# An attention, expert-attention and mixing kernel on one core: one 128-row piece of the theta weights is handed to a later stage of the order

## The chip, the cores and the metric

The program runs on one core of one Trainium2 chip. The metric is the device time of the execution in microseconds; the median of three runs is compared. The core has TensorE (PE, with its weight loads shown apart as PEld), VectorE (DVE), ScalarE (ACT), GpSimd (POOL) and SyncE (SP), whose queue issues most of the transfers. Each engine works through its own instructions in the order in which they stand in its queue.

## The reference

Three layers follow one another, for 4 batches of 576 tokens and 512 channels:

```
x  = local attention of 8 heads of 64, each query sees the last 64 keys
x  = for each of 4 experts: causal attention over x, times wo[e]; each token takes its best 2 experts
theta = x @ w_theta
y  = w_tok_r @ (x * cos(theta)) + w_tok_i @ (x * sin(theta))
u  = x + y
out = u + max(u @ w_ch, 0)
```

The weights of the last layer (w_theta, w_tok_r and w_tok_i, w_ch) come as 64-bit floats, since they are scaled in the host's double precision; the kernel receives their bits and turns them into a pair of 32-bit numbers, high and low, whose sum carries the value.

## The kernel before

Batches 0 to 3 go through local attention (`phase_a`), the projections to queries, keys, values and gates (`qk`, `vg_gates`), expert attention (`attn(b, ep)`, ep being the pair of experts 0, 1 or 2, 3) and, last, the mixing layer (`theta`, `mix` or `mix7`, `channel`). While one batch is in `attn`, `phase_a` and `qk` of the next ones run between its pieces. `merge` interleaves generators: each yields a cost, and the one that has the smallest share of its total done goes next. For each batch there are two such merges, the first half with `attn(b, 0)` and the second with `attn(b, 1)`. The build then schedules each engine's order from what `merge` emitted, so that a piece that is emitted elsewhere also moves its neighbours.

The table `THS` says in which half of which batch a 128-row piece c of the theta weights is handed to `load_theta` (lines 830 to 836): entry 2b is the first half of batch b, entry 2b + 1 the second. `load_theta` takes two 128-row buffers of the tag `zc` (the raw 64-bit piece `w64t` of 512 KB, and the scratch `wtut`), and calls `load64` (lines 107 to 148), which issues for each piece, in this order of dependence:

- SP, L115: one transfer of the raw piece, queued behind the last key tile `kt`
- POOL, L124: the high words scaled; ACT, L129: the low words scaled
- DVE, L130: a shift; DVE, L136: sign bit and shifted bits joined, with `w64t` and `wtut` as its two inputs
- POOL, L138: the sum of the two parts as integers
- ACT, L146: the high result `wth`; DVE, L147: the low result `wtl`, with `wtut` and `wth` as inputs

The results are read by the matmuls of `fuse`, at 277 us of the profiled execution. Nothing else reads them.

Other lines that the prediction speaks of: `pool_mul` (L87), the POOL copies of queries into `QD` and of keys into `KA`; L279, the score matmuls `as` of local attention; L284 the masked reduction of `as` on DVE; L299 the POOL multiplication that normalises `ams`; L452 the masked reduction of expert scores on DVE; L469 the scaling of `bms` and its diagonal part `bpd`, on POOL or DVE; L480 and L486 the transposes `bpt` and `bdt` of these on PE; L484, L482 and L490 their copies to `bpT`. Names carry the batch first: `as200` is batch 2, head pair 0, group 0; `bms011` is batch 0, expert pair 1, tile 1.

Of the kernel before, what the change touches and what calls it, by code (L numbers as in the profile page):

```python
# [28 lines left out]
CT = ("tb", "bs")  # L29
WARM = 2  # L30
TK0 = 1
THS = [[], [0], [], [1], [2], [3], [], []]
NB = S // 64
NC = DM // P
BIG = 1.0e30
# [22 lines left out]
def kernel(ctx, tc, qT, kT, vw, consts, w_in, w_o, w_th, w_tk, w_ch, outT):  # L58
# [143 lines left out]
    def load_w(src, n, dst_h, dst_l, tag):  # L202
        for c in range(n):
            h, l = dst_h(c), dst_l(c)
            pool, home = (cp, "zc") if tag == "zc" or tag == "both" and c >= 2 else (bp, "bms")
            st = pool.tile([P, h.shape[1]], F32, tag=home, bufs=2, name=f"wst{c}")
            with tc.issue_after(last_load[0].ins):
                nc.sync.dma_start(st, src[c * P : (c + 1) * P])
            w = h.shape[1]
            eh, el = KN["WE"][{"zc": 2}.get(tag, 0 if w == W0 else 1)]  # L210
            cut = w * eh // 4
            if eh < 4:
                nc.scalar.copy(out=h[:, cut:], in_=st[:, cut:])
            if eh > 0:
                nc.vector.tensor_copy(out=h[:, :cut], in_=st[:, :cut])
            cut = w * el // 4
            if el < 4:
                nc.gpsimd.tensor_sub(out=l[:, cut:], in0=st[:, cut:], in1=f32(h[:, cut:]))
            if el > 0:
                nc.vector.tensor_sub(out=l[:, :cut], in0=st[:, :cut], in1=f32(h[:, :cut]))  # L220
            yield 0.1
# [284 lines left out]
    def wo(b):  # L506
        for n0, n1 in ((0, 320), (320, 576)):
            for m in range(NC):
                g = bank([P, n1 - n0], ("gggg", ("as", "ta", "g", "g"), ("as", "g", "ta", "g"))[KN["WB"][b]][m], f"x2{b}{m}{n0}")
                for c in range(2):  # L510
                    oh, ol = O[b, c]
                    mm3(g, woh[c][:, m * P : (m + 1) * P], wol[c][:, m * P : (m + 1) * P],
                        oh[:, n0:n1], ol[:, n0:n1], c == 0, c == 1)
                nc.scalar.copy(out=x2T[b][:, m, n0:n1] if b < 2 else xs[b][m // 2][:, m % 2, n0:n1], in_=g)
                if b > 1 and n1 == S and m % 2:
                    nc.sync.dma_start(xd[b][:, m - 1 : m + 1], xs[b][m // 2])
                yield 0.75
# [312 lines left out]
    def load_theta(cs):  # L830
        for c in cs:
            st = cp.tile([P, DM], U64, tag="zc", bufs=2, name=f"w64t{c}")
            tu = cp.tile([P, 2, DM], U32, tag="zc", bufs=2, name=f"wtut{c}")
            load64(0, st, tu, wth[:, c], wtl[:, c], w_th[c * P : (c + 1) * P],
                   1.0 / TWO_PI)
            yield 1.0
# [48 lines left out]
    for b in range(B):  # L885
# [5 lines left out]
        if b > 0:  # L891
            todo.append((KN["WO"][b - 1], wo(b - 1)))
        if THS[2 * b]:
            todo.append((KN["TW"][0] * len(THS[2 * b]), load_theta(THS[2 * b])))
        if b == 3:
# [21 lines left out]
        if KN["WOI"] == 2 * b + 1:  # L917
            todo.append((KN["CW"][6], load_w(w_o, 2, lambda c: woh[c], lambda c: wol[c], "zc")))
        if THS[2 * b + 1]:
            todo.append((KN["TW"][1] * len(THS[2 * b + 1]), load_theta(THS[2 * b + 1])))  # L920
        if b == 2:
# [93 lines left out]
```

## Time and profile before

| | us |
|---|---|
| median of 3 runs | 509.3 (507.8 to 509.64) |
| the profiled execution's own time | 506.32 |
| its span | 504.5 |
| PE busy in the span | 480.7 (95%) |
| PEld, DVE, ACT, POOL busy | 446.4, 373.6, 346.4, 328.4 |
| granted TensorE clock | 0.999 of full speed |

The profiled execution took 3.0 us less than the median of the runs. Busy shares are averages over the whole span; the stretch from 60 to 110 us, in which the change moves work, is read by itself in the section on the rows. A matmul's record covers its passage through the array and overlaps the next one's, so PE can show as busy while its order holds back; PEld shows such stretches better.

### The profile page before, as it was taken

The page shows a single profiled execution, that of the slowest core. Times are in us where ns is not written, and L with a number is a line of the kernel's source. Part 1 is how long each engine was busy: PE and PEld are TensorE (multiplying, and loading weights), DVE is VectorE, ACT ScalarE, POOL GpSimd, SP SyncE. Part 2 cuts the span into 40 slices and gives each one's busy share as a digit, 9 for nine tenths or more (in the row PEclk, how much of TensorE's full clock was granted, in tenths as well). Part 3 has the DMA queues.
Part 4 walks back from the last instruction along what each step waited for, and adds up shares of the span by engine and source line. Part 5 has one row for each costly group of instructions (what it writes and reads, how often), then busy time and mean ns, then how long its engine had stood idle before and what let it go on. Part 6 is the DMA issues. An engine that isn't in the chain of part 4 may idle for free.

```text
span 504.5 us, 12104 instructions
## 1 busy us (share of the span) xinstructions
PE 480.7 (95%) x4128; PEld 446.4 (88%) x4128; DVE 373.6 (74%) x1274; ACT 346.4 (69%) x1072; POOL 328.4 (65%) x455
## 2 busy tenths in 40 slices
PE   7798999999999999999999989999999999999997
PEld 5688888889998999988878778899998999999997
DVE  5766887865977868845897778987769948894942
ACT  7948787866787868858696797886177727652620
POOL 6758899764685772335784367579658926891770
PEclk9999999999999999999999999999999999999999
DMA  7564233431335342111246953231272044202002
GB/s 256 189 212 155 83 123 114 130 114 64 122 88 177 124 141 78 34 47 49 52 146 208 318 166 142 55 93 43 76 196 64 23 142 131 64 23 95 1 0 95
DMA packets 45470, 55.92 MB, mean 111 GB/s; under 512 B 6497, under 2 KB 34145, under 8 KB 45409
## 3 DMA queue, kind: packets, MB, share of 16 engines
q1 hardware_dynamic: 44544, 52.46, 33.1%
q10 hardware_dynamic: 864, 2.69, 1.5%
q8 instruction: 33, 0.54, 0.4%
q14 instruction: 29, 0.23, 0.2%
HBM read 43.34 MB, written 11.80 MB: 109 GB/s over the span
## 4 chain that ended last, share of the span: by engine, by line
PE 51%; DVE 20%; ACT 11%; POOL 9%; issue 5%; DMA 4%; SPq 0%; POOLq 0%; DVEq 0%; ACTq 0%
PE as L279 4%; PE bpt L480 3%; PE qk L100 2%; PE c L100 2%; DMA w64k<-in_dram 2%; PE qk L101 2%; PE apt L304 2%; PE c L102 2%; PE qk L102 2%; PE c L101 2%; ACT ams L292 2%; PE ao L159 2%; DMA wst<-in_dram 2%; PE bs L448 2%; DVE ang L656 2%
## 5 line engine op out<-in xcount | busy, mean ns | idle before, releaser
L292 ACT ACTIVATE ams<-ams,anm 128x128 f32<-128x128 f32 x144 | 56.6, 396 | 6.1 <-DVE anm L284 4.8
L299 POOL TENSOR_TENSOR ams<-ams,arc 128x384 f32<-128x384 f32 x48 | 40.1, 836 | 24.9 <-DVE arc L298 15.5
L87 POOL TENSOR_SCALAR QD<-qt 64x192 f32<-64x192 f32 x72 | 40.1, 557 | 19.1 <-PE as L279 11.6
L457 ACT ACTIVATE bms<-bms,bnm 64x64 f32<-64x64 f32 (+4 forms) x80 | 44.8, 562 | 9.3 <-DVE bnm L452 8.8
L279 PE MATMUL as<-kt,QD 128*128 128x128 f32 x288 | 41.9, 282 | 3.9 <-DVE anm L284 1.5
L284 DVE CUSTOM_DVE_ANT_0 ams<-as,cst 128x128 f32<-128x128 f32 x144 | 35.0, 284 | 11.5 <-PE apt L304 7.8
L279 PEld LDWEIGHTS as<-kt,QD 128*128 128x128 f32 x288 | 36.6, 193 | 7.4 <-ACT x0h L94 1.5
L452 DVE CUSTOM_DVE_ANT_0 bms<-bs,mb 64x64 f32<-64x64 f32 (+4 forms) x80 | 32.6, 424 | 7.5 <-PE bs L450 4.7
L469 POOL TENSOR_SCALAR bpd<-bms,bsm,gw 128x64 f32<-128x64 f32 (+1 forms) x47 | 21.9, 467 | 23.1 <-DVE bsm L462 10.6
L97 POOL TENSOR_TENSOR cu<-x2T,cu 128x288 fp32r<-128x288 f32 x32 | 29.1, 923 | 7.3 <-ACT cu L94 7.3
L100 PE MATMUL y<-wkh,z 128*128 128x288 f32 x108 | 32.1, 302 | 0.2 <-DVE x2T L694 0.2
L448 PE MATMUL bs<-KA,QS 128*128 128x288 f32 (+4 forms) x96 | 31.8, 340 | 0.4 <-DVE bnm L452 0.2
L101 PE MATMUL y<-wkl,z 128*128 128x288 f32 x108 | 31.9, 297 | 0.0
L102 PE MATMUL y<-wkh,z 128*128 128x288 f32 x108 | 31.3, 297 | 0.0
L768 POOL TENSOR_TENSOR x2T<-x2T,u 128x288 f32<-128x288 f32 x20 | 16.6, 839 | 21.3 <-DVE u L779 11.1
L480 PE MATMUL bpt<-cst,bms 128*128 128x128 f32 x160 | 27.6, 278 | 2.9 <-POOL bms L469 1.8
L648 ACT ACTIVATE ang<-th,magic 128x256 f32<-128x256 f32 x36 | 16.7, 466 | 17.9 <-PE th L102 17.5
L656 DVE TENSOR_TENSOR ang<-xk,ang 128x512 f32<-128x512 f32 x32 | 21.7, 684 | 8.2 <-ACT ang L653 6.2
L450 PE MATMUL bs<-KL,QS 128*128 128x288 f32 (+4 forms) x96 | 27.6, 295 | 0.1
L292 ACT ACTIVATION_READ_ACCUMULATOR ams<-ams,anm 128x1 f32 x144 | 27.5, 191 | 0.0
L820 DVE SCALAR_TENSOR_TENSOR x2T<-c,x2T 128x288 f32<-128x288 f32 x32 | 13.9, 453 | 16.5 <-PE c L102 16.3
L469 POOL TENSOR_SCALAR bms<-bms,bsm,gw 128x384 f32<-128x384 f32 (+3 forms) x40 | 25.4, 636 | 0.0
(336 smaller groups left out, 2040.5 us busy)
## 6 DMA issues: line engine op xcount, KB each, us to landing
vt<-in_dram SPq DMA_DIRECT2D x48, 192.0 KB, 3.1
or<-od SPq DMA_DIRECT2D x32, 256.0 KB, 3.3
kt<-in_dram SPq DMA_DIRECT2D x15, 320.0 KB, 3.1
qt<-in_dram SPq DMA_DIRECT2D x16, 288.0 KB, 3.4
out_dram<-x2T SPq DMA_DIRECT2D x32, 144.0 KB, 1.8
w64k<-in_dram SPq DMA_DIRECT2D x5, 576.0 KB, 3.7
od<-oh SPq DMA_DIRECT2D x8, 288.0 KB, 3.2
od<-ol SPq DMA_DIRECT2D x8, 288.0 KB, 4.1
```

Source lines behind the costliest of these rows:

```text
L87: nc.gpsimd.tensor_scalar(out=out, in0=in_, scalar1=by, scalar2=1.0, op0=ALU.mult, op1=ALU.mult)
L100: nc.tensor.matmul(out, wh, xh, start=first, stop=False)
L101: nc.tensor.matmul(out, wh, xl, start=False, stop=False)
L102: nc.tensor.matmul(out, wl, xh, start=False, stop=last)
L279: nc.tensor.matmul(s[:, i, :], QD[g][:, i], kt[:, 64 * blk : 64 * blk + 128], start=True, stop=True)
L284: nc.vector.tensor_tensor_reduce(out=ms[:, i, :], in0=s[:, i, :], in1=ma0 if (g == 0 and i == 0) else ma1, scale=-0.125, scalar=3.0e38, op ...
L292: nc.scalar.activation(out=ms[:, i, :], in_=ms[:, i, :], func=AF.Exp, bias=nm[:, i : i + 1], scale=-1.0, accum_out=sm[:, i, 0:1],)
L299: nc.gpsimd.tensor_mul(out=ms, in0=ms, in1=rc.unsqueeze(2).to_broadcast([P, 3, P]))
L448: nc.tensor.matmul(s[:m, : z - a], qs[:, q0 : q0 + m], ka[:, a:z], start=True, stop=False)
L457: ex = nc.scalar.activation(out=ms[:m, :w], in_=ms[:m, :w], func=AF.Exp, bias=nm[:m, ci : ci + 1], scale=-1.0, accum_out=ss[:m, i, 0:1])
L469: eng.tensor_scalar(out=dst, in0=src, scalar1=sm[:m, i : i + 1], scalar2=gw[:m, t, 2 * ep + i : 2 * ep + i + 1], op0=ALU.mult, op1=ALU.mult)
L480: nc.tensor.transpose(pt[:, jj, i, :], pn[:, i, P * j : P * j + P], ident)
```

## The change

The piece c = 0 is emitted with the first half of batch 1 and no longer with the second half of batch 0. The pieces 1, 2 and 3 stay where they were.

```
-THS = [[], [0], [], [1], [2], [3], [], []]
+THS = [[], [], [0], [1], [2], [3], [], []]
```

The program has the same instructions before and after. What moves is their order on each engine. On SP, around the transfer of piece 0 (`w64t0`; `kt`, `qt`, `vt` are keys, queries and values of local attention), before:

```order
L246 DMA kt20_1573<-in_1_dram 128x640
L115 DMA w64t0_1602<-in_6_dram 128x512
L247 DMA qt21_2053<-in_0_dram 128x576
L260 DMA vt122_1192<-in_2_dram 128x384
L260 DMA vt130_1280<-in_2_dram 128x384
L246 DMA kt21_2054<-in_1_dram 128x640
L260 DMA vt131_1342<-in_2_dram 128x384
```

and now:

```order
L246 DMA kt20_1573<-in_1_dram 128x640
L247 DMA qt21_2043<-in_0_dram 128x576
L260 DMA vt122_1192<-in_2_dram 128x384
L260 DMA vt130_1280<-in_2_dram 128x384
L246 DMA kt21_2044<-in_1_dram 128x640
L115 DMA w64t0_2081<-in_6_dram 128x512
L260 DMA vt131_1342<-in_2_dram 128x384
```

The transfer moved four places down, from behind `kt20` to behind `kt21`.

On POOL, the place where piece 0 was converted, before (L124 and L138 are its two instructions):

```order
L469 TENSOR_SCALAR bms002_1218<-bms002_1218,bsm002_1219,gw0_921 128x256
L124 TENSOR_SCALAR wtut0_1603<-w64t0_1602 128x512
L87 TENSOR_SCALAR QD0_105<-qt20_1572 64x3x64 x2
L469 TENSOR_SCALAR bpd003_1370<-bms003_1368,bsm003_1369,gw0_921 128x64
...
L299 TENSOR_TENSOR ams122_1200<-ams122_1200,arc122_1208 128x384
L87 TENSOR_SCALAR QD1_106<-qt20_1572 64x3x64 x2
L138 TENSOR_TENSOR wtut0_1603<-wtut0_1603 128x512
L299 TENSOR_TENSOR ams130_1288<-ams130_1288,arc130_1296 128x384
```

and the place where it is converted now:

```order
L299 TENSOR_TENSOR ams131_1350<-ams131_1350,arc131_1358 128x384
L469 TENSOR_SCALAR bpd010_1519<-bms010_1517,bsm010_1518,gw0_921 64x64
L124 TENSOR_SCALAR wtut0_2082<-w64t0_2081 128x512
L87 TENSOR_SCALAR QD0_105<-qt21_2043 64x3x64 x2
L299 TENSOR_TENSOR ams132_1397<-ams132_1397,arc132_1405 128x384
L138 TENSOR_TENSOR wtut0_2082<-wtut0_2082 128x512
L469 TENSOR_SCALAR bpd011_1689<-bms011_1687,bsm011_1688,gw0_921 128x64
L469 TENSOR_SCALAR bms011_1687<-bms011_1687,bsm011_1688,gw0_921 128x128
```

Both instructions stand later, among the tiles 0 and 1 of batch 0's second expert pair, and three instructions lie between them where there were nine.

On ACT, the place to which L129 of piece 0 moves; the rows are those of the changed kernel:

```order
L94 CAST oh00_1009<-o003_1444 128x128
L292 ACTIVATE ams132_1397,AS0_114<-ams132_1397,anm132_1398 128x128
L129 ACTIVATE wtut0_2082<-w64t0_2081 128x512
L484 COPY bpT004_1483<-bpt0040_1484 128x512
L457 ACTIVATE bms011_1687,BS3_121<-bms011_1687,bnm021_1690 128x192
L309 COPY apv122_1216<-apt122_1212 128x384
```

Before, the copy to `bpT004` stood right behind the cast to `oh00`; L129 now stands in front of it. On DVE, L130 stands now in front of the three reductions of `ams200`, and L136 behind them and one reduction of `bms012`. On all engines but SP, neighbours change places by some rows from here to about 390 us of the profiled execution; behind that the orders are the same.

## Rows read from the trace of the kernel before

**Rows 1.** The page, busy time, share of the span and instructions by engine.
```profile
PE 480.7 (95%) x4128; PEld 446.4 (88%) x4128; DVE 373.6 (74%) x1274; ACT 346.4 (69%) x1072; POOL 328.4 (65%) x455
```

**Rows 2.** Windows by stage: length, busy us by engine (instructions), clock, DMA share, GB/s.
```profile
72.00:84.40 12.40, 11.61 (x128) 9.28 (x126) 10.16 (x53) 10.33 (x41) 12.05 (x20) 1.00 0.32 95
84.40:95.00 10.60, 10.55 (x103) 8.99 (x104) 8.54 (x45) 8.35 (x34) 8.99 (x17) 1.00 0.52 167
110.00:225.00 115.00, 114.97 (x1125) 107.08 (x1124) 84.67 (x400) 86.78 (x311) 64.76 (x113) 1.00 0.29 95
225.00:300.00 75.00, 70.26 (x557) 61.28 (x555) 58.48 (x187) 59.08 (x158) 45.25 (x59) 1.00 0.49 161
```

**Rows 3.** Timeline of POOL, 60 to 95 us: start, us, instruction [idle before, releaser].
```profile
60.47 0.76 POOL L469 TENSOR_SCALAR bpd<-bms,bsm,gw 64x64 f32<-64x64 f32 x2 [1.58 <-DVE arc L298]
...
72.90 0.68 POOL L124 TENSOR_SCALAR wtut<-w64t 128x512 f32<-128x512 f32 x1
...
75.00 0.86 POOL L469 TENSOR_SCALAR bpd<-bms,bsm,gw 128x64 f32<-128x64 f32 x1
...
76.49 0.39 POOL L469 TENSOR_SCALAR bpd<-bms,bsm,gw 128x64 f32<-128x64 f32 x1
...
79.51 1.27 POOL L138 TENSOR_TENSOR wtut<-wtut 128x512 int32<-128x512 int32 x1
...
81.56 0.89 POOL L469 TENSOR_SCALAR bpd<-bms,bsm,gw 128x64 f32<-128x64 f32 x1
...
86.34 0.39 POOL L469 TENSOR_SCALAR bpd<-bms,bsm,gw 64x64 f32<-64x64 f32 x1
86.69 1.15 POOL L87 TENSOR_SCALAR QD<-qt 64x192 f32<-64x192 f32 x2
87.92 0.83 POOL L299 TENSOR_TENSOR ams<-ams,arc 128x384 f32<-128x384 f32 x1
88.74 0.43 POOL L469 TENSOR_SCALAR bpd<-bms,bsm,gw 128x64 f32<-128x64 f32 x1
...
90.05 1.16 POOL L87 TENSOR_SCALAR QD<-qt 64x192 f32<-64x192 f32 x2 [0.45 <-PE as L279]
...
94.85 0.83 POOL L299 TENSOR_TENSOR ams<-ams,arc 128x384 f32<-128x384 f32 x1 [0.57 <-DVE arc L298]
```

**Rows 4.** Timeline of DVE, 74 to 89 us.
```profile
74.07 0.42 DVE L130 TENSOR_SCALAR wtut<-wtut 128x512 uint32<-128x512 uint32 x1
...
74.90 0.69 DVE L136 SCALAR_TENSOR_TENSOR wtut<-w64t,wtut 128x512 uint32<-128x512 uint32 x1
...
81.49 0.69 DVE L147 SCALAR_TENSOR_TENSOR wtl<-wtut,wth 128x512 fp32r<-128x512 f32 x1
...
86.93 0.29 DVE L284 CUSTOM_DVE_ANT_0 ams<-as,cst 128x128 f32<-128x128 f32 x1
...
88.99 0.48 DVE L452 CUSTOM_DVE_ANT_0 bms<-bs,mb 128x320 f32<-128x320 f32 x1
```

**Rows 5.** Timeline of ACT, 72 to 85 us.
```profile
72.50 0.66 ACT L129 ACTIVATE wtut<-w64t 128x512 uint32<-128x512 uint32 x1
...
80.82 0.63 ACT L146 ACTIVATE wth<-wtut 128x512 fp32r<-128x512 f32 x1
...
85.01 0.58 ACT L484 COPY bpT<-bpt 128x512 f32<-128x512 f32 x1 [1.59 <-PE bpt L480]
```

**Rows 6.** Timeline of SP's transfers, 68 to 81 us.
```profile
68.02 0.38 SPq L115 DMA_DIRECT2D w64t<-in_dram  x1
...
80.47 0.33 SPq L246 DMA_DIRECT2D kt<-in_dram  x1
```

**Rows 7.** Tile w64t over the whole span: durations ns min/median/max, and landing of its transfers.
```profile
L136 DVE SCALAR_TENSOR_TENSOR wtut<-w64t,wtut x4: 691/692/1195, 74.9 to 180.3; 128x512 uint32<-128x512 uint32 x4
...
DMA to landing us min/median/max: 3.6/4.1/4.4
```

**Rows 8.** Timeline of PE, the transposes that wait for POOL, at 83 us.
```profile
83.25 0.33 PE L480 MATMUL bpt<-cst,bms 128*128 128x128 f32 x1 [0.29 <-POOL bms L469]
```

## The prediction

> **What bounds the kernel now.** I read the page's busy shares first: PE is busy for 95% of the span [rows 1], so whatever keeps PE from issuing is what counts, and work on the other engines counts only through PE. Then I read the windows by stage, since an average hides where PE waits. From 110 to 225 us PE is busy for 114.97 of 115 us while POOL needs 64.76 [rows 2]: there PE sets the pace, and work of the other engines can be moved about. From 225 to 300 us PE is idle for 75.00 - 70.26 = 4.74 us [rows 2]. The stretch of the change, 72 to 84.4 us, is another thing again: POOL is busy for 12.05 of 12.40 us, and PEld for 9.28 only [rows 2]. The timeline of POOL says why: from 60.47 us on it works without a wait worth a mark until 90.05 us (idle 0.45 before it) and 94.85 us (0.57) [rows 3], and where PE waits, it waits for a scaling on POOL (`bpt` at 83.25 us, 0.29 us [rows 8]). So from 60 to about 95 us POOL is the engine that sets the pace, and behind that it is PE.
>
> **What the change removes from its old place.** Piece 0 is converted between 72.5 and 82.2 us, inside that stretch.
> - POOL: L124 for 0.68 us and L138 for 1.27 us [rows 3], together 1.95 us. There is a second part. A scaling `bpd` takes 0.39 us at 76.49, but 0.86 us at 75.00, when DVE is in L136 (from 74.90 for 0.69 us [rows 4]), and 0.89 us at 81.56, when DVE is in L147 (from 81.49 for 0.69 us) [rows 3, 4]. Both POOL instructions were held up, by 0.47 and 0.50 us. So piece 0 costs POOL 1.95 + 0.97 = 2.92 us.
> - DVE: 0.42 + 0.69 + 0.69 = 1.80 us [rows 4]. ACT: 0.66 + 0.63 = 1.29 us [rows 5]. SP: one issue of 0.38 us [rows 6].
>
> POOL's next instructions at the old place come up to 2.92 us earlier, and with them the `bms004` for which PE waits. I count on that lead until about 84 us.
>
> **What it adds at the new place.** The new place on POOL is behind the `bpd010` that ends at 86.34 + 0.39 = 86.73 us [rows 3]. It still lies in the stretch that POOL fills: the move is by twelve microseconds, not by half a batch. From 72 to 95 us POOL has 12.05 + 8.99 = 21.04 us of work [rows 2], the same work before and after. With the lead, `bpd010` ends at 86.73 - 2.92 = 83.81 us. From there I walk POOL on:
> - L124 waits for the transfer. It is issued behind `kt21`, at 80.47 + 0.33 = 80.80 us if nothing came earlier [rows 6], and lands 3.6 to 4.4 us later [rows 7], so at 84.4 to 85.2 us: a wait of 0.6 to 1.4 us. If `kt21`, which needs the scores before it to have been read, comes earlier by the L130 and L136 that DVE no longer has there (0.42 + 0.69 = 1.11 us [rows 4]), the wait is 0 to 0.3 us. I take the middle of the ends, 0.7 us. Behind L124 on POOL are `QD0`, `ams132` and all later scalings, for which PE waits.
> - L124 takes 0.68 us, `QD0` and the gap behind it 87.92 - 86.69 = 1.23 us, `ams132` 88.74 - 87.92 = 0.82 us [rows 3].
> - L138 waits for L136. From the end of L124, DVE does L130 (0.42), three reductions of `ams200` (0.29 each), one of `bms012` (0.48) and L136 (0.69), 2.46 us [rows 4]. POOL has 1.23 + 0.82 = 2.05 us to do meanwhile, so it waits 0.4 us; if `bs0220`, `as200` or L136 itself is late, more. The longest L136 took 1195 ns where the median is 692 [rows 7], which makes 0.9 us.
> - L138 takes 1.27 us.
>
> In sum `bpd011` starts at 83.81 + 0.7 + 0.68 + 1.23 + 0.82 + 0.4 + 1.27 = 88.9 us, and it started at 88.74 us [rows 3]: POOL has lost the whole lead where it is past the piece. The ends are 87.8 us with no wait (0.9 us early) and 90.1 us with both waits at their longest, 1.4 and 0.9 us (1.4 us late). The 0.45 and 0.57 us that POOL idles by 94.85 us [rows 3] take up 1.0 us of a delay. L147 may again hold one POOL instruction by 0.5 us, as before, now inside that slack.
>
> The hold is a rule of the Trainium skill. "SBUF — State Buffer", section "SBUF: two separate sides", says that a DVE instruction with two inputs in SBUF and a GpSimd instruction that reads SBUF exclude each other, and that the one that starts first keeps the ports to its end. This trace agrees for L136 and L147 (0.86 and 0.89 us against 0.39). The rule speaks against the change: at the new place the neighbour of L136 on POOL is `ams132`, 0.83 us long, and if that starts first, L136 waits for its end and L138 for L136, so that by the rule the sum would come out up to 0.8 us later on POOL, inside the late end above.
>
> On ACT, L129 now stands in front of the copy to `bpT004`. ACT was idle for 1.59 us before that copy, from 83.42 us [rows 5], so the 0.66 us are hidden if the piece has landed by 84.35 us. With the landings above (84.4 to 85.2 us, or 1.1 us earlier) the copy starts between 84.0 and 85.9 us, against 85.01: from 1.0 us earlier to 0.9 us later. I take 0; the middle is within 0.1 us of it.
>
> Elsewhere the change only permutes neighbours, up to about 390 us. Their price isn't in the trace. Where PE is full (110 to 225 us) I take nothing; from 225 to 300 us the 4.74 us of PE's idle time [rows 2] bound a gain, and nothing excludes a loss of the same size. I take 0, as the same instructions wait for the same work, and half of the bound, 2.4 us either way, for the range.
>
> **The sum** is 0 within -0.9 to +1.4 us on POOL, 0 on ACT, 0 elsewhere: the profiled execution stays at 506.3 us. The median of the runs is 3.0 us above that, so I forecast **509.3 us**. A measurement here can tell about 0.5%, 2.5 us, from no change, so faster means under 506.8 and slower over 511.8 us.
>
> **Rivals.**
> - *PE keeps the lead* (faster). Until 84 us POOL is 2.92 us ahead. If PE uses that and the work that POOL brings late between 84 and 95 us isn't yet needed, PE enters its full stretch earlier and stays so, since nothing else bounds it there. For it: `ams200` and `QD1` have time before PE reads them. Against: `bms011` and `bms012`, also behind L138, are transposed at once. It gives 509.3 - 2.9 = 506.4 us. Chance 0.26.
> - *The transfer comes late* (slower). ACT stops at L129, POOL at L124, L138 at L136; the copy to `bpT004` is 0.9 us late, POOL 1.4 us, and PE, which goes on in order, meets one after the other: 509.3 + 2.3 = 511.6 us, and with the permuted neighbours going against it up to 514.0. It decides at the landing: after 84.4 us the copy to `bpT004` is later than before. For it: three in-order engines wait where before the piece lay ready as ACT and POOL reached it. Against: SP's `kt21` itself should come earlier. Chance 0.26, of which half is over 511.8 us.
> - *The permuted neighbours decide*, from 225 to 300 us, where DVE is busy for 58.48 and PE for 70.26 of 75 us [rows 2]. Either sign, 2.4 us and more: 506.9 or 511.7 us and beyond. Chance 0.18, half to each side, and of that three quarters past the bound of 0.5%.
> - *It doesn't do what it says*: the piece moves by twelve microseconds, inside the same stretch. That is my forecast, and no case of its own.
>
> **How the numbers follow.** The forecast has 0.30. Of the first rival 0.22 pass the lower bound, since the lead is just larger than 2.5 us; of the second 0.15 (half, and what adds to it from the permutations); of the third 0.07 to each side. Faster 0.29, slower 0.22, same 0.49 would follow; I move 0.05 from same to slower, as a third wait behind the two was not priced. So faster 0.29, same 0.44, slower 0.27. The range goes from 509.3 - 2.9 - 1.9 = 504.5 us (the lead kept and most of the 2.4 us gained) to 511.6 + 2.4 = 514.0 us.
>
> **What would show it.** Right: in the changed kernel POOL shows no L124 between 72 and 84 us, `bpd` beside no L136 takes 0.39 us, POOL's L124 starts near 84.4 us and `bpd011` within 1 us of 88.9 us, and PE is busy in 110 to 225 us as before. Wrong: PE ahead by over 2 us at 110 us with the lead kept to the end (first rival); ACT idle before L129 on the transfer and `bpT004` after 85.5 us (second); equal times at 225 us and a difference of over 2 us at 300 us (third).

## The result and the profile after

The changed kernel takes 511.5 us (median of 12 runs, 510.1 to 514.7), the kernel before beside it 508.0 us (12 runs, 506.7 to 510.2): ratio 1.0062 [1.0042, 1.0083]. Two more comparisons, below, gave 1.0076 and 1.0077. It is slower by some 0.7%, about 3.5 us. The profiled execution is 512.1 us long with a span of 510.3 us.

The page of the changed kernel, answering to [rows 1]:

```profile
PE 481.5 (94%) x4128; PEld 448.3 (88%) x4128; DVE 377.0 (74%) x1274; ACT 346.4 (68%) x1072; POOL 329.1 (64%) x455
```

The busy times hardly moved (PE 480.7 to 481.5 us); the span did, so PE stands still or works slowly somewhere. The windows of the changed kernel say where. The columns are those of [rows 2]; the last three are new:

```profile
60.00:72.00 12.00, 10.40 (x86) 9.27 (x85) 9.44 (x48) 9.06 (x36) 9.68 (x20) 0.86 0.24 66
...
72.00:84.40 12.40, 11.89 (x119) 10.18 (x121) 8.61 (x56) 10.78 (x43) 10.06 (x19) 1.00 0.33 99
84.40:95.00 10.60, 10.15 (x117) 8.70 (x117) 9.96 (x43) 8.63 (x36) 9.49 (x15) 1.00 0.55 185
110.00:225.00 115.00, 112.45 (x1099) 105.10 (x1098) 84.67 (x393) 84.97 (x308) 65.45 (x111) 1.00 0.31 99
225.00:300.00 75.00, 70.97 (x590) 62.16 (x589) 60.91 (x193) 57.97 (x158) 44.78 (x61) 1.00 0.47 156
...
165.00:170.00 5.00, 5.00 (x50) 4.59 (x50) 3.49 (x18) 2.80 (x10) 4.83 (x10) 1.00 0.92 299
170.00:175.00 5.00, 4.46 (x41) 4.02 (x40) 4.29 (x19) 4.68 (x16) 3.29 (x5) 1.00 0.04 13
175.00:180.00 5.00, 3.69 (x45) 3.27 (x45) 3.32 (x15) 4.61 (x18) 4.54 (x7) 1.00 0.53 174
```

The same 15 us in the kernel before, in one row:

```profile
165.00:180.00 15.00, 15.00 (x147) 14.30 (x147) 11.59 (x54) 13.10 (x46) 13.12 (x21) 1.00 0.31 98
```

The stretch that was full, 110 to 225 us, now has 2.55 us without PE, and 1.86 us of that lie between 165 and 180 us (5.00 + 4.46 + 3.69 of 15). That is 80 us behind the new place of piece 0. What PE waits for there (engine and line, waited for, us in total, times, longest):

```profile
PE qk L100 <- ACT vg L372: 1.3, 1, 1.3
PE vg L100 <- DVE QS L355: 0.5, 1, 0.5
```

The chain of waits of the changed kernel follows these back (start, us, what):

```profile
162.72 6.33 DMA w64t<-in_dram
...
...
169.90 0.78 ACT ams L292 x4
...
172.38 0.69 DVE wtut L136
...
173.66 0.87 ACT bms L457 x2
...
175.68 0.52 ACT wth L146
...
176.65 0.39 ACT vg L372
...
177.07 0.40 PE qk L100
```

It is a transfer of `w64t`, but not of piece 0: it is piece 2, which the diff doesn't touch. ACT comes to its L129 and stands until it has landed, 6.33 us after its issue, where [rows 7] had 4.4 us at most; behind L129 in ACT's row lie the cast to `oh`, the exponentials and the copies that PE needs. SP's issues show one reason for the late landing. In the changed kernel:

```profile
161.77 0.42 SPq L503 DMA_DIRECT2D od<-oh  x1
162.29 0.38 SPq L503 DMA_DIRECT2D od<-ol  x1
162.72 0.49 SPq L115 DMA_DIRECT2D w64t<-in_dram  x1
```

and in the kernel before:

```profile
157.44 0.38 SPq L115 DMA_DIRECT2D w64t<-in_dram  x1
...
160.57 0.42 SPq L503 DMA_DIRECT2D od<-oh  x1
161.09 0.38 SPq L503 DMA_DIRECT2D od<-ol  x1
```

The new order puts two stores in front of piece 2: SP's row changes here too, which the description of the change had said of the other engines only. But ACT's wait itself is hardly longer than it was. Its timeline in the changed kernel:

```profile
169.07 0.67 ACT L129 ACTIVATE wtut<-w64t 128x512 uint32<-128x512 uint32 x1 [1.24 <-DMA w64t<-in_dram]
```

and in the kernel before:

```profile
161.12 0.70 ACT L129 ACTIVATE wtut<-w64t 128x512 uint32<-128x512 uint32 x1 [0.99 <-DMA w64t<-in_dram]
```

Before, ACT waited 0.99 us there and PE lost nothing: L129 stood behind the exponentials of `ams302` and two copies, with the cast of a finished `oh` next. Now it stands eight instructions later on ACT, between the first and the second of the three exponentials of `ams310`, and the wait of 1.24 us lies on PE's path, with the piece's own steps in the chain behind it (L129, from 169.11 to 169.65, L136 and L146: 0.54 + 0.69 + 0.52 = 1.75 us).

How long ACT waits does not decide. In `r_after`, a second execution of the changed kernel, its timeline of ACT shows a shorter wait than the kernel before had:

```profile
167.46 0.67 ACT L129 ACTIVATE wtut<-w64t 128x512 uint32<-128x512 uint32 x1 [0.88 <-DMA w64t<-in_dram]
```

In `e7_piece1_early`, a run of the next section in which piece 2 keeps its old place, the wait is longer than in either kernel:

```profile
166.14 0.69 ACT L129 ACTIVATE wtut<-w64t 128x512 uint32<-128x512 uint32 x1 [1.66 <-DMA w64t<-in_dram]
```

By the table that follows, `r_after` loses 2.6 us at this place all the same, and `e7_piece1_early` nothing.

To see where a kernel loses or gains, I compare traces at equal work. PE does the same 4128 matmuls in every kernel of this study; each form of matmul gets one duration (from the kernel before), these are added up in the order of each trace, and I read off how far a kernel is behind the first trace of before once it has done as much. The table has the change of that lag over five stretches, in us (plus: time lost), and the whole measurement. An end that falls among rows in another order can shift a value by some tenths, at 280 us and in the middle of rows that changed places by up to 1 us. The last column also holds falls of the granted clock, which the text takes up at its end. One of the 12 executions of `e5_late_pair_before` took 1575.5 us; its ratio leaves that one out.

```
run                    80-125  125-165  165-180  180-280  280-460  ratio to before
r_before                 0.0     +0.1      0.0      0.0     +0.1   1.0013
after                   -0.8     +0.1     +2.8     -0.3     +1.3   1.0062
r_after                 -0.9     +0.1     +2.6     -0.3     +1.2   1.0076
r_after5                -0.8     +0.1     +2.8     -0.2     +3.4   1.0077
e8_convert_behind       -0.8     +0.1     +0.3     +0.4     +0.6   1.0014
e4_late_pair_after      -0.8     +0.1     +0.7     +1.7     -2.2   1.0013
e5_late_pair_before      0.0      0.0     +0.3     +2.0     +1.9   1.0027
e7_piece1_early         +1.8     +0.1      0.0     -0.3     +2.0   1.0044
e3_fetch_early          -0.9     +2.1     +0.8     +0.1     +2.5   1.0076
e1_store_behind         -0.9     +0.1     +2.0     +0.8     +8.5   1.0220
e2_store_ahead           0.0     +0.6     +0.2     +1.6     +6.7   1.0197
e10_convert_last        -0.8     +0.1     +1.5     +1.4     +8.5   1.0189
```

So in the changed kernel piece 0 at its new place gains 0.8 us, in each of its traces, and 2.6 to 2.8 us go at 165 to 180 us.

### The profile page after: what moved, and what is told of

Read it like the earlier page. It is cut to its first block, busy times and chain, and to the rows that moved or that the text cites. A ratio compares the mean times of both kernels' runs of the same rounds, so it can differ in the third digit from the quotient of the medians.

```text
span 510.3 us, 12104 instructions
## 1 busy us (share of the span) xinstructions
PE 481.5 (94%) x4128; PEld 448.3 (88%) x4128; DVE 377.0 (74%) x1274; ACT 346.4 (68%) x1072; POOL 329.1 (64%) x455
## 4 chain that ended last, share of the span: by engine, by line
PE 43%; DVE 25%; ACT 13%; POOL 6%; issue 6%; DMA 6%; SPq 0%; POOLq 0%; DVEq 0%; ACTq 0%
PE as L279 4%; ACT ams L292 2%; PE c L100 2%; PE c L102 2%; PE c L101 2%; PE apt L304 2%; PE qk L100 2%; DMA wst<-in_dram 2%; PE bpt L480 2%; PE qk L101 2%; PE qk L102 2%; DVE ang L614 2%; PE ao L159 2%; PE bs L448 2%; DVE ang L656 2%
## 5 line engine op out<-in xcount | busy, mean ns | idle before, releaser
L279 PE MATMUL as<-kt,QD 128*128 128x128 f32 x288 | 43.5, 286 | 4.0 <-ACT x0h L94 1.3
L469 POOL TENSOR_SCALAR bpd<-bms,bsm,gw 128x64 f32<-128x64 f32 (+1 forms) x47 | 20.8, 444 | 20.8 <-DVE bsm L462 9.8
L87 POOL TENSOR_SCALAR KA<-KA 64x288 fp32r<-64x288 f32 x32 | 15.5, 484 | 17.4 <-ACT KA L357 15.0
L480 PE MATMUL bpt<-cst,bms 128*128 128x128 f32 x160 | 26.2, 275 | 0.4 <-DVE bms L469 0.4
```

The source lines that it names most:

```text
L87: nc.gpsimd.tensor_scalar(out=out, in0=in_, scalar1=by, scalar2=1.0, op0=ALU.mult, op1=ALU.mult)
L279: nc.tensor.matmul(s[:, i, :], QD[g][:, i], kt[:, 64 * blk : 64 * blk + 128], start=True, stop=True)
L469: eng.tensor_scalar(out=dst, in0=src, scalar1=sm[:m, i : i + 1], scalar2=gw[:m, t, 2 * ep + i : 2 * ep + i + 1], op0=ALU.mult, op1=ALU.mult)
L480: nc.tensor.transpose(pt[:, jj, i, :], pn[:, i, P * j : P * j + P], ident)
```

## The experiments

**Both kernels again, and the two stores.** First I took the order of SP's row for the cause: the transfer of piece 2 behind two stores. One run undoes that in the changed kernel, one makes it in the kernel before. In the next four texts theory A is that piece 2's transfer is late because of the stores, B that piece 0's own new place costs the time, C that the permuted neighbours do and no one place.

`r_before` is the kernel before under its own name, and measures the method.

> The kernel before, once more, for a second profile. Every theory: ratio to before 1.000 within 0.003. Its trace shows how much of the difference between the two traces is scatter: TensorE's clock fell to 0.86 in 60 to 72 us of the changed kernel's trace, ahead of any moved instruction, and if that is scatter, the lag of about 2 us at 70 us is absent or stands elsewhere here.

`r_after` is the changed kernel.

> The changed kernel, once more, for a second profile. Every theory: ratio 1.006 (1.003 to 1.009). Theory A (the loss is made at 160 to 180 us, by the transfer of theta piece 2, which SP now issues behind the two stores of batch 1's first expert pair, and on which ACT's L129 waits in line): the lag behind the kernel before grows by 2 to 3 us between 160 and 180 us again, and w64t of piece 2 lands over 5 us after its issue. Theory B (the loss is made where piece 0 is converted now, 80 to 100 us): it grows there. Theory C (permuted neighbours, no one place): it grows at other places than in the first trace.

`e1_store_behind`:

```
-                nc.sync.dma_start(st, src)
+                theta_dma[0] = nc.sync.dma_start(st, src)
...
-                nc.sync.dma_start(od[b][:, 2 * ep + k], f32(x))
+                if (b, ep) == (1, 0):
+                    held.append((od[b][:, 2 * ep + k], x))
+                else:
+                    nc.sync.dma_start(od[b][:, 2 * ep + k], f32(x))
...
+            if c == 2:
+                with tc.issue_after(theta_dma[0].ins):
+                    for dst, x in held:
+                        nc.sync.dma_start(dst, f32(x))
```

> The changed kernel with the two stores of batch 1's first expert pair (od1 from oh10 and ol10) issued behind the transfer of theta piece 2 again, as in the kernel before; engines' orders are those of the changed kernel up to about 158 us. Theory A: the loss goes, ratio to before 1.000 (0.996 to 1.003). Theory B: it stays, 1.006 (1.004 to 1.009), since everything up to 158 us is unchanged. Theory C: between the two or beyond, with no rule.

`e2_store_ahead`, an edit of the kernel before:

```
-            with tc.issue_after(last_load[0].ins):
+            with tc.issue_after(last_load[0].ins), tc.issue_after(stored[1, 0].ins) if kind == 0 and gate[0] else nullcontext():
                 nc.sync.dma_start(st, src)
...
-                    nc.sync.dma_start(od[b][:, 2 * ep + k], f32(x))
+                    stored[b, ep] = nc.sync.dma_start(od[b][:, 2 * ep + k], f32(x))
...
+            gate[0] = c == 2
```

> The kernel before with the transfer of theta piece 2 held until the two stores of batch 1's first expert pair are issued, piece 0 untouched; orders are those of the kernel before up to about 158 us. Theory A: the loss comes, ratio 1.004 to 1.008, with ACT idle on the transfer at L129 of piece 2. Theory B: 1.000 (0.997 to 1.003). Theory C: anything from 0.996 to 1.008.

Measured: `r_before` 1.0013 [0.9990, 1.0035], `r_after` 1.0076 [1.0049, 1.0103], `e1_store_behind` 1.0220 [1.0182, 1.0259], `e2_store_ahead` 1.0197 [1.0168, 1.0227]. Both edits cost 2%, so theory A fails as I had put it. The table shows two things. At 165 to 180 us, `e1` still loses 2.0 us with the transfer in front of the stores, and `e2` nothing with it behind them: the stores are not what decides. And both lose 7 to 9 us behind 280 us, where the edit does nothing but leave the rows in another order. Windows of `e1_store_behind` there:

```profile
285.00:290.00 5.00, 2.23 (x14) 1.63 (x12) 1.63 (x5) 2.38 (x6) 0.00 (x0) 1.00 0.60 216
290.00:295.00 5.00, 4.25 (x18) 3.75 (x19) 5.00 (x15) 4.26 (x11) 3.04 (x2) 0.68 0.89 264
```

and its timeline of ACT:

```profile
287.62 0.72 ACT L127 ACTIVATE wtuk<-w64k 128x576 f32<-128x576 f32 x1 [4.80 <-DMA w64k<-in_dram]
```

There ACT stands in front of a 64-bit piece again, one of the token weights: it waits 4.80 us of the 6.17 us from that transfer's issue to its landing. PE runs dry (2.23 us of 5), and the granted clock falls behind the gap (0.68 as the mean of the second row), and once more later (0.66 at 305 to 310 us). So the stores are not the mechanism; what the two places have in common is an engine that stands in line for a 64-bit piece. Theory B fails too: 80 to 125 us gains.

**Earlier, or not there at all.** The next runs move the pieces. "Late piece" is the theory that remains; "own place" is B, "order" is C.

`e3_fetch_early`, an edit of the changed kernel (set for piece 2 alone):

```
-            with tc.issue_after(last_load[0].ins):
+            with nullcontext() if ungate[0] and kind == 0 else tc.issue_after(last_load[0].ins):
                 nc.sync.dma_start(st, src)
```

> The changed kernel with one edit: piece 2's transfer no longer stands behind the last token loads, so SyncE issues it nine places earlier, before both stores of batch 1's first pair; the orders are those of the changed kernel up to about 130 us and again from about 225 us on. Late piece (ACT's L129 stands in line for piece 2, whose transfer took 6.0 us from its issue at 161.5 us, and 2.7 us of PE are lost at 165 to 175 us): that loss goes, the 0.8 us lost near 440 us stays, ratio to before 1.002 (1.000 to 1.004). Own place (piece 0's new home at 80 to 100 us costs the time): stays at 1.006 to 1.008. Order (any other order of the rows loses as much somewhere): 1.005 or more, with the loss at another place.

`e4_late_pair_after`:

```
-THS = [[], [], [0], [1], [2], [3], [], []]
+THS = [[], [], [0], [1], [], [2], [3], []]
```

> The changed kernel with pieces 2 and 3 half a batch later each, so no piece is fetched or converted at 160 to 180 us. Late piece: the 2.7 us at 165 to 175 us are not lost; 0.998 to 1.003 of before unless pieces 2 and 3 make ACT wait at their new places. Against the run of the kernel before with the same two pieces moved (the next one), whose orders are the same beyond about 188 us: 0.8 us less, ratio of the two 0.998 (0.996 to 1.001). Own place: 1.006 of the next run. Order: the two may differ by 1% either way, since their rows between 60 and 188 us are in different orders.

`e5_late_pair_before`, against the kernel before:

```
-THS = [[], [0], [], [1], [2], [3], [], []]
+THS = [[], [0], [], [1], [], [2], [3], []]
```

> The kernel before with pieces 2 and 3 half a batch later each; orders as before up to about 158 us, other rows from there to 390 us. Late piece: nothing was lost to piece 2 before, so 1.000 (0.998 to 1.003) unless the two pieces make ACT wait at their new places. Own place: 1.000. Order: up to 1.02, as the two runs in which only two stores changed places with one fetch showed, with a loss at 270 to 310 us.

`e7_piece1_early`, against the kernel before:

```
-THS = [[], [0], [], [1], [2], [3], [], []]
+THS = [[], [0], [1], [], [2], [3], [], []]
```

> The kernel before with piece 1, not piece 0, moved by half a batch: from the second half of batch 1 into its first half, where the change puts piece 0. Orders differ from before only between about 85 and 141 us. Late piece: no loss at 165 to 175 us, since piece 2 stands as before; 1.000 (0.998 to 1.002). Own place (a piece at 80 to 100 us costs POOL and DVE time there): 1.004 to 1.006. Order: a loss of 1 us or more between 85 and 141 us.

Measured: `e3` 511.3 us, 1.0076 [1.0048, 1.0105]; `e4` 507.6 us, 1.0013 [0.9988, 1.0039]; `e5` 509.1 us, 1.0027 [1.0007, 1.0048]; `e7` 509.8 us, 1.0044 [1.0027, 1.0062].

In `e4` piece 0 stands where the change puts it, piece 2 comes later, and PE is busy throughout the stretch of the loss. Its window:

```profile
165.00:180.00 15.00, 15.00 (x149) 14.16 (x149) 9.46 (x46) 11.57 (x41) 11.01 (x19) 1.00 0.38 123
```

The stretch isn't free of the piece, as the expectation had it: ACT stands for 1.95 us before L129 of piece 2, which starts at 179.31 us. That is longer than in the changed kernel, and PE, busy until 190 us, loses 0.91 us between 190 and 195 us. Again the place counts, and not the length of the wait.

`e4` and `e5` differ only in piece 0's place and in rows up to about 188 us; their intervals overlap, so that pair says no more than that piece 0's move isn't what costs 0.7%.

`e3` missed. The transfer would have been in time for the old place, but the build put the conversion earlier as well, and 2.1 us went there instead. Its window, and its chain of waits:

```profile
145.00:150.00 5.00, 3.53 (x25) 2.74 (x24) 3.65 (x16) 4.25 (x15) 4.27 (x8) 1.00 0.03 12
```

```profile
144.21 1.29 POOL wtut L138
...
145.53 0.64 ACT wth L146
...
146.20 0.99 DVE wtl L147
...
147.63 1.26 ACT ams L293 x6
```

No transfer stands in this chain (ACT's L129 of piece 2 began at 140.00 us without a wait): POOL, ACT and DVE do the piece's steps one behind the other, and ACT's exponentials come after them. `e7` is like it, but for a wait of 1.25 us that ACT had before L129 of piece 1 (87.31 us): L136 and L147 of piece 1 stand in its chain at 91.7 and 95.4 us. Its 1.8 us between 80 and 125 us met the number of "own place" (1.0044 of 1.004 to 1.006), but with piece 1: a second piece right behind piece 0. So the conversion alone can cost 2 us, as `e3` shows, while piece 0 costs nothing at its new place. "Late piece" is too narrow as a rule for any place; for the changed kernel its place in the row had still to be tested without moving the transfer.

**The conversion behind the copy.** `e8_convert_behind` leaves SP's row and the transfer alone and ties one instruction on ACT to a later place (fifteen places later in the order that was built); the build moves neighbours of it up to about 225 us:

```
-            nc.scalar.copy(out=vg[:w, i, :], in_=g[:w])
+            vgc[b, i] = nc.scalar.copy(out=vg[:w, i, :], in_=g[:w])
...
-            with tc.issue_after(closed[0].ins) if kind == 2 else nullcontext():
+            with tc.issue_after(closed[0].ins) if kind == 2 else tc.issue_after(pin[0].ins) if pin[0] else nullcontext():
                 nc.scalar.mul(out=u, in_=lo, mul=2.0**-29)
...
+            pin[0] = vgc[2, 1] if c == 2 else None
```

> The changed kernel with one edit: ACT's L129 of piece 2 goes behind the copy of batch 2's second V and gate tile (L372), twelve places later in ACT's row; SyncE's row, the transfer and its place behind the two stores stay. Orders differ from the changed kernel only between about 158 and 225 us. Late piece (ACT standing at L129 for the transfer, with the copies that PE needs behind it): ACT no longer waits for piece 2 and PE keeps the 2.7 us at 165 to 175 us; ratio to before 1.001 to 1.003, against the changed kernel 0.995. Conversion (the piece's work on DVE, POOL and ACT costs PE the same wherever it stands between 160 and 180 us): the loss comes some us later, 1.006. Own place: 1.006.

`e10_convert_last` has `vgc[2, 3]` in place of `vgc[2, 1]`.

> As the run before, but L129 of piece 2 behind the fourth such copy, 29 places later than in the changed kernel (some 15 us). Orders then differ from 158 us to about 300 us. Late piece: no loss at 165 to 175 us; piece 3 comes later too, and the token weights behind it at 270 to 300 us; 1.000 to 1.003 if they land in time, up to 1.02 if they don't, as in the two runs with the stores exchanged. Conversion: 1.006 or more, with a loss at 178 to 190 us. Own place: 1.006.

And the changed kernel ran again beside them:

> The changed kernel again, beside the two runs before on the same chip: 1.006 to 1.008 of before by every theory; the profile again shows PE idle for 1.6 us or more at 170 to 180 us and no loss at 80 to 115 us.

Measured: `e8` 508.3 us, 1.0014 [0.9988, 1.0040]; the changed kernel 511.6 us, 1.0077 [1.0053, 1.0102]; `e10` 517.6 us, 1.0189 [1.0165, 1.0213]. The first two intervals lie apart. `e8` at the place, windows:

```profile
165.00:180.00 15.00, 15.00 (x147) 14.03 (x147) 11.87 (x51) 13.45 (x44) 12.89 (x21) 1.00 0.46 157
```

its timeline of SP:

```profile
160.84 0.38 SPq L505 DMA_DIRECT2D od<-ol  x1
161.26 0.48 SPq L115 DMA_DIRECT2D w64t<-in_dram  x1
```

and its timeline of ACT:

```profile
173.21 0.38 ACT L374 COPY vg<-vg 128x260 f32<-128x260 f32 x1
173.48 0.67 ACT L129 ACTIVATE wtut<-w64t 128x512 uint32<-128x512 uint32 x1
```

The transfer is still behind both stores, and it still takes up to 5.8 us to land. The piece is still converted at this place: DVE has 11.87 us of work in the window where the changed kernel has 3.49 + 4.29 + 3.32 = 11.10. But ACT does the copy `vg` first, at 173.21 us where the changed kernel had it at 176.65, L129 waits for no transfer, and PE is busy for all 15 us. So what costs 2.4 of the 2.7 us is L129's place in ACT's row, in front of the exponentials that PE needs. The piece's step on DVE stayed where it was, in front of the reductions of `ams311`; the timeline of DVE:

```profile
169.81 0.69 DVE L136 SCALAR_TENSOR_TENSOR wtut<-w64t,wtut 128x512 uint32<-128x512 uint32 x1
```

What left the front of ACT's row is the wait (1.24 us), L129 itself (0.54 us in the chain) and L146 (0.52 us; it now starts at 178.92 us), together 2.30 us. Other rows moved with them, so this run alone doesn't exclude that some of those helped; `e4`, in another order, loses as little PE time at this place. How much of the 2.4 us is the wait and how much ACT's two steps isn't shown; `e3`, without a wait, shows that the steps alone can cost 2.1 us at another place.

`e10` overdoes it. At 165 to 180 us PE stays busy (14.93 of 15 us, though the table puts 1.5 us there, across rows in another order), but piece 3 and the token weights come later and land later, and the end of the chain is `e1`'s again:

```profile
282.03 6.53 DMA w64k<-in_dram
```

I found no version that beats both kernels: the best, `e4` and `e8`, are level with the kernel before.

## Why the prediction was wrong

I forecast no change, 509.3 us, with a range of 504.5 to 514.0 us and 0.27 for slower by over 0.5%. It is slower by 0.6 to 0.8%. By its own steps:

- **The new place of piece 0: right in its sum.** The clock fell at 60 to 72 us in the profiled execution after, so I read the steps in `e3_fetch_early`, whose rows are in the same order up to 130 us, whose clock stayed at 1.00 and which was level with the kernel before within 0.1 us at 74 us. Its timeline of POOL:

```profile
83.82 0.39 POOL L470 TENSOR_SCALAR bpd<-bms,bsm,gw 64x64 f32<-64x64 f32 x1
84.18 0.67 POOL L124 TENSOR_SCALAR wtut<-w64t 128x512 f32<-128x512 f32 x1
...
86.31 0.83 POOL L300 TENSOR_TENSOR ams<-ams,arc 128x384 f32<-128x384 f32 x1
87.82 1.27 POOL L138 TENSOR_TENSOR wtut<-wtut 128x512 int32<-128x512 int32 x1 [0.69 <-DVE bsm L462]
89.09 0.43 POOL L470 TENSOR_SCALAR bpd<-bms,bsm,gw 128x64 f32<-128x64 f32 x1
```

  and its timeline of ACT and of DVE:

```profile
83.78 0.68 ACT L129 ACTIVATE wtut<-w64t 128x512 uint32<-128x512 uint32 x1 [1.19 <-DMA w64t<-in_dram]
84.36 0.58 ACT L485 COPY bpT<-bpt 128x512 f32<-128x512 f32 x1
```

```profile
86.78 0.90 DVE L136 SCALAR_TENSOR_TENSOR wtut<-w64t,wtut 128x512 uint32<-128x512 uint32 x1
```

  I had said: L124 near 84.4 us (84.18), POOL idle for 0.4 to 0.9 us before L138 (0.69), `bpd011` at 88.9 us (89.09), the copy to `bpT004` between 84.0 and 85.9 us (84.36). `r_after`, whose clock stayed at 1.00 too, shows the same steps 1.6 us later (85.76 us for L124, 90.68 for `bpd011`), as it was that far behind at 74 us already. That the sum came out so near is in part luck, as two terms were off and nearly cancel: `bpd010` ended at 84.21 us and not at 83.81, and L124 then waited for nothing, where I had put 0.7 us. `kt21` was issued at 79.51 us, 0.96 us earlier than before; that is the earlier of my two cases, and I had taken the middle. The old place gave its lead, `bpd` beside no L136 takes 0.39 us again, and PE came out 0.8 us ahead, inside my ends. The hold between DVE and POOL came in the direction in which "SBUF — State Buffer" of the Trainium skill, section "SBUF: two separate sides", has it: `ams132` starts first (86.31 us, 0.83 long), and L136 takes 0.90 us where the median was 0.69 [rows 7]. It cost 0.2 us, not the 0.8 that I had allowed for, and less than the 0.36 us that `ams132` still had to run when L136 began.

- **"Elsewhere the change only permutes neighbours … Where PE is full (110 to 225 us) I take nothing": this step failed.** I read a full stretch as one with room for anything. It is full because nothing stands in line there; POOL's 64.76 us of 115 [rows 2] are slack of POOL, not of ACT's row. ACT already waited for piece 2 in the trace before, at no cost: PE was busy for all 15 us. The permutation brought L129 in front of exponentials that PE needs: 2.7 us, where I had taken 0. The later landing (6.33 us against 4.4 at most [rows 7]) is not what decides: ACT's wait grew by 0.25 us in the profiled execution and was shorter than before in `r_after` (0.88 us against 0.99), which loses as much. It is the third rival's mechanism at a place that I had excluded, and neither 225 us nor 300 us was the mark to look at.

- **The transfer of piece 0 comes late** (second rival): it did not decide. ACT did wait 1.19 us before L129, but `bpT004` came in time.

- **PE keeps the lead** (first rival): it kept 0.8 us of the 2.9, up to 165 us.

- **The sum that remains.** -0.8 + 2.7 leaves 1.9 of some 3.5 us. Another 1.2 to 1.3 us come behind 280 us in `after` and `r_after`, 0.8 us of it at 435 to 440 us, as in `r_after5` and in `e5`. In `r_after5` it is 3.4 us, and there the granted clock fell to its lower level behind a gap at 288 to 292 us (0.59 as the mean of 292 to 296 us): some 1.6 us, an estimate from 0.41 of these 4 us. ACT's longest wait for the token weights is 2.2 us there, 1.3 us in the other two and 0.9 us in the kernel before. Why the change brings the 0.8 us, I have not settled.

## What to carry to other kernels

When a moved piece shifts the order that the build chooses, look downstream for every instruction that belongs to background work, above all those that wait on a transfer, and ask in both orders what stands behind it on its engine: a stretch in which the bounding engine is full is no stretch with room for that. How long the instruction waits told little here; what stands behind it told more. Where it costs, move that instruction behind the work that the bounding engine needs, rather than the transfer; and expect that a larger shift opens the same hole further on.

## What the hardware showed that I had not expected

The same program reaches the same hole with two outcomes. At 62 to 64 us PE is idle for some 1.5 of 2 us. In the changed kernel's first trace the clock fell to its lower level, 1.2 GHz (0.50 in the third row), behind it:

```profile
62.00:64.00 2.00, 0.42 (x3) 0.14 (x1) 1.86 (x11) 1.56 (x5) 2.00 (x5) 1.00 0.28 109
64.00:66.00 2.00, 1.99 (x12) 1.95 (x13) 1.91 (x9) 1.98 (x9) 1.85 (x5) 0.73 0.00 0
66.00:68.00 2.00, 2.00 (x10) 1.93 (x9) 1.22 (x10) 1.91 (x10) 1.73 (x5) 0.50 0.00 0
```

In `r_after`, the same kernel, it did not:

```profile
62.00:64.00 2.00, 0.50 (x4) 0.13 (x1) 1.82 (x10) 1.55 (x6) 2.00 (x5) 1.00 0.31 120
64.00:66.00 2.00, 1.92 (x14) 1.86 (x15) 1.87 (x9) 1.98 (x9) 1.84 (x5) 1.00 0.00 0
```

From 60 to 70 us the lag grows from 0.9 to 2.9 us in the first trace and from 1.0 to 1.5 us in `r_after`, so the fall costs some 1.5 us. It came in four of the thirteen traces, of both kernels and of one edit (`r_before`, `after`, `r_after5` and `e7`). A fall behind the gap at 288 to 292 us came in seven (`r_after5`, `e1`, `e2`, `e3`, `e5`, `e7` and `e10`). The runs of the kernel before lie 3.5 us apart (506.7 to 510.2), so a reader who compares two single traces can take such a fall for an effect of the change. It isn't what makes the changed kernel slower: of the executions whose granted clock is 1.000 over the whole span, those of the changed kernel took 511.2 us (median of 7) and those of the kernel before 507.2 us (median of 34).
